# Seven-product blocks for one more unit, three wide sums for eight narrow ones, and output halves added in DRAM

## The chip, the cores and the metric

One NeuronCore of one Trainium2 chip runs the whole program. The metric is device time in microseconds (us). The kernel before takes 655.93 us, the median of three runs (655.39 to 657.26). In the text PE is the matrix engine, DVE the vector engine, ACT the scalar engine, POOL the GpSimd engine and SP the engine whose queue issues nearly all DMAs.

## The reference, cut to what matters

For each of 8 batches and 8 heads, 512 tokens `x` and 32 state rows attend to each other in both directions; the result, 4352 rows of 512, goes through a feed-forward block with a hard-swish:

```
xread = softmax(x @ state.T / 8) @ state        # 8 x 8 heads, 512 tokens
sread = softmax(state @ x.T / 8) @ x            # 8 x 8 heads, 32 rows
t = concat([xread, sread]) as (4352, 512)
h = t @ w_in                                    # (4352, 2048)
g = h * clip(h + 3, 0, 6) / 6
out = g @ w_out                                 # (4352, 512), float32
```

## The kernel before, in words

The hidden width 2048 is taken in two sweeps of 1024, that is 8 blocks of 128 each. A **unit** is one sweep over one batch's 512 tokens, or over the 256 rows of all `sread` (b = 8): 18 units of 8 **steps**. Unit order before: sweep 0 with b = 0 to 8, then sweep 1 with b = 0 to 8. Step n makes one 128-row block of h in a PSUM bank (`first`, tile `ps_h`, two banks): six matmuls of 512 columns, because every float32 factor is kept as a high and a low part and three products of parts are summed. ACT then writes relu(h + 3) (L1162 or L1177) and DVE multiplies min(that, 6) by h (L1164 or L1179).

What follows a step comes in two kinds. In a **plain** unit (`second`) g is split into high and low (`split`, L379 on ACT and L380 on DVE), and four row tiles are multiplied by a block of `w_out`: 4 x 3 matmuls of 512 columns a step (L988), summed over 8 steps in PSUM banks `acc0` to `acc3`. In a **seven-product** unit (`seven(k)`: sweep 1, b = 1 to 7) two g blocks and two row tiles form a 2 x 2 block matrix, multiplied by seven half-size products for eight (`seconds`): 7 x 3 matmuls of 256 columns a step (L1077). Four `w_out` combinations are made once (`combine`, in sweep 1's unit b = 0). For each step DVE makes four 128-wide sums and differences of quarters of G (L1045), and the quarters (tile `g_hi`, `g_lo`) and three sums (tile `tmp`) are split. A unit has two passes (q = 0, 1) of four steps, two row tiles each; at the end of a pass the four banks are joined: ACT copies acc0 and part of acc1 out to `tops` (L1090, L1091), DVE adds three pieces into `ot` (L1094, L1097), POOL adds the rest in four instructions (L1100), and SP stores the half to `out` (L1112).

`ot` holds 1/6 of the sum over both sweeps: sweep 0 stores its part to a DRAM buffer (`part`, L1248) and sweep 1 loads it back (`load_part`, L1197). The two `sread` units are treated so too, the second one as the last unit of all.

The order of instructions is worked out while the program is built: `Plan` holds every operation with an engine, a cost, a rank (the table `RANKS`), dependencies and buffer slots, and lays them out engine by engine (`order`); engines run their rows strictly in that order. Idle transposes (L1433) fill the gaps of PE up to the first step.

Of the kernel before, what the change touches and what calls it, by code (L numbers as in the profile page):

```python
# [1463 lines left out]
```

## Time and profile before

| | before |
|---|---|
| median of 3 runs | 655.93 us |
| the profiled execution | 656.56 us, of which the span from first to last instruction 654.2 us |
| PE / DVE / ACT / POOL busy | 98% / 81% / 51% / 10% of the span |
| DMA | 82.00 MB moved |

The profiled execution lies 0.63 us above the median. Busy PE is not PE at its peak, since matmuls overlap: what tells is from which start to which start they come, and what an idle PE waited for. The stretch from 400 to 640 us is sweep 1 with its seven-product units; 120 to 400 us is most of sweep 0, the first `sread` unit and the one plain unit of sweep 1.

### The profile page before, as it was taken

What the parts mean: (1) busy time and instruction counts of PE and PEld (TensorE: products, weight loads), DVE (VectorE), ACT (ScalarE), POOL (GpSimd) and SP (SyncE); (2) the same over time, 40 slices, a digit from 0 to 9 for tenths busy, and PEclk for the clock granted to TensorE, in tenths of its full rate; (3) what the DMA queues carried; (4) which work ended last, traced back from release to release, by engine and by line L of the source; (5) the groups of instructions that cost most, each with busy time, mean ns of one, the idle gap of its engine ahead of it and who ended that gap; (6) DMA issues with size and microseconds to landing.
All of it is one profiled execution on the core that took longest, in us unless ns stands there. A gap on an engine that the chain in (4) does not pass through costs nothing.

```text
span 654.2 us, 11536 instructions
## 1 busy us (share of the span) xinstructions
PE 638.1 (98%) x4383; PEld 514.9 (79%) x4383; DVE 530.1 (81%) x1023; ACT 331.9 (51%) x591; POOL 63.3 (10%) x63
## 2 busy tenths in 40 slices
PE   8999998999999999999999999999999999999997
PEld 7446776867777868777897877988898889898996
DVE  4989779887979859788479557899899989899973
ACT  4848444554545634546355444454555454464531
POOL 0000000000000000000000000123121422313122
PEclk9999999999999999999999999999999999999999
DMA  9985796887859557333313032305040404020102
GB/s 288 266 188 148 126 223 105 247 168 182 173 149 225 126 145 176 88 74 141 90 65 134 32 134 76 123 33 181 18 166 34 165 33 166 34 97 33 65 34 64
DMA packets 147007, 82.00 MB, mean 125 GB/s; under 512 B 124808, under 2 KB 134536, under 8 KB 144776
## 3 DMA queue, kind: packets, MB, share of 16 engines
q1 hardware_dynamic: 146808, 81.01, 45.1%
q8 instruction: 34, 0.56, 0.3%
q10 hardware_dynamic: 144, 0.26, 0.2%
q14 instruction: 21, 0.17, 0.1%
HBM read 50.84 MB, written 26.74 MB: 119 GB/s over the span
## 4 chain that ended last, share of the span: by engine, by line
PE 79%; DVE 11%; SPq 4%; DMA 3%; issue 2%; ACT 1%; DVEq 0%; ACTq 0%
PE ps_h L988 26%; PE acc L988 25%; PE acc L1077 18%; PE ps_s L604 3%; PE acc L1212 2%; DVE g_lo L380 2%; SPq L591 2%; PE ps_s L988 2%; PE ps_h L604 1%; PE ps_h L1143 1%; SPq L559 1%; DVE g L1045 1%; DVE tmp L380 1%; DMA raw<-in_moe_w_in_dram 1%; DMA raw<-in_x_dram 1%
## 5 line engine op out<-in xcount | busy, mean ns | idle before, releaser
L988 PE MATMUL acc<-w_out_hi,g_hi 128*128 128x512 f32 x288 | 115.6, 401 | 0.9 <-ACT g_hi L379 0.9
L988 PE MATMUL acc<-w_out_hi,g_lo 128*128 128x512 f32 x288 | 112.3, 390 | 0.0
L988 PE MATMUL acc<-w_out_lo,g_hi 128*128 128x512 f32 x288 | 112.3, 390 | 0.0
L1177 ACT ACTIVATE g<-ps_h,three 128x512 f32<-128x512 f32 (+1 forms) x88 | 57.0, 649 | 78.9 <-PE ps_h L988 76.7
L1179 DVE SCALAR_TENSOR_TENSOR g<-g,ps_h 128x512 f32<-128x512 f32 (+1 forms) x88 | 55.7, 634 | 40.5 <-ACT g L1177 40.0
L1077 PE MATMUL acc<-w_out_hi,tmp 128*128 128x256 f32 x336 | 88.0, 283 | 0.0
L988 PE MATMUL ps_h<-aT_hi,wp_hi 128*128 128x512 f32 (+1 forms) x232 | 85.0, 366 | 2.4 <-DVE wp_lo L380 1.3
L988 PE MATMUL ps_h<-aT_lo,wp_hi 128*128 128x512 f32 (+1 forms) x232 | 83.8, 361 | 0.0
L988 PE MATMUL ps_h<-aT_hi,wp_lo 128*128 128x512 f32 (+1 forms) x232 | 83.5, 360 | 0.0
L1100 POOL TENSOR_TENSOR tops<-tops 128x256 f32<-128x256 f32 x28 | 23.5, 838 | 549.9 <-DVE g L1045 415.9
L379 ACT CAST g_hi<-g 128x512 fp32r<-128x512 f32 (+1 forms) x84 | 48.5, 579 | 46.7 <-PE acc L988 24.8
L988 PEld LDWEIGHTS acc<-w_out_hi,g_hi 128*128 128x128 f32 x288 | 54.1, 188 | 20.8 <-issue 6.9
L380 DVE TENSOR_TENSOR g_lo<-g,g_hi 128x512 fp32r<-128x512 f32 (+1 forms) x84 | 53.7, 640 | 19.8 <-ACT g_hi L379 17.3
L1077 PE MATMUL acc<-w_out_hi,g_lo 128*128 128x256 f32 x224 | 63.8, 285 | 1.7 <-DVE g_lo L380 1.7
L1077 PEld LDWEIGHTS acc<-w_out_hi,tmp 128*128 128x128 f32 x336 | 64.4, 192 | 0.1
L1077 PE MATMUL acc<-w_out_hi,g_hi 128*128 128x256 f32 x224 | 64.0, 286 | 0.3 <-DVE ot L1094 0.3
L988 PEld LDWEIGHTS acc<-w_out_hi,g_lo 128*128 128x128 f32 x288 | 54.1, 188 | 12.0 <-DVE g_lo L380 0.6
L1077 PE MATMUL acc<-w_out_lo,g_hi 128*128 128x256 f32 x224 | 63.4, 283 | 0.0
L988 PEld LDWEIGHTS acc<-w_out_lo,g_hi 128*128 128x128 f32 x288 | 54.1, 188 | 11.5 <-issue 1.1
L1162 ACT ACTIVATE G<-ps_h,three 128x512 f32<-128x512 f32 x56 | 38.4, 688 | 43.5 <-PE ps_h L988 43.5
L988 PEld LDWEIGHTS ps_h<-aT_hi,wp_hi 128*128 128x128 f32 x232 | 43.8, 189 | 11.2 <-issue 1.8
L988 PEld LDWEIGHTS ps_h<-aT_hi,wp_lo 128*128 128x128 f32 x232 | 43.8, 189 | 6.9
(153 smaller groups left out, 1273.1 us busy)
## 6 DMA issues: line engine op xcount, KB each, us to landing
part<-ot SPq DMA_DIRECT2D x8, 1024.0 KB, 4.7
ot<-part SPq DMA_DIRECT2D x8, 1024.0 KB, 6.9
raw<-in_x_dram SPq DMA_DIRECT2D x112, 64.0 KB, 3.3
xb<-in_x_dram SPq DMA_DIRECT2D x28, 256.0 KB, 4.8
out_dram<-ot SPq DMA_DIRECT2D x14, 512.0 KB, 2.8
raw<-in_moe_w_out_dram SPq DMA_DIRECT2D x11, 511.8 KB, 5.4
raw<-in_moe_w_in_dram SPq DMA_DIRECT2D x8, 511.0 KB, 5.1
raw<-raw SPq DMA_DIRECT2D x112, 32.0 KB, 2.0
```

The lines of the kernel that those rows point to most:

```text
L379: S_(cost, rank, lambda: nc.scalar.copy(hi(), src()), reads, [writes[0]])
L380: V(cost, rank, lambda: nc.vector.tensor_tensor(lo(), src(), hi().bitcast(F32), op=ALU.subtract), [*reads, writes[0]], [writes[1]])
L559: nc.sync.dma_start(x_tile(b, read)[:, :, j, :], x_v[b, j])
L591: nc.sync.dma_start(t[rows, i].rearrange("t (a c) -> t a c", c=NS), x[b, 4 * g + 2 * i + u, :, k * NS : (k + 1) * NS].rearrange("(a t) c - ...
L604: nc.tensor.matmul(out[u][cols, :], made["stT", b][rows, cols], moving(q)[rows], start=True, stop=True,)
L988: nc.tensor.matmul(ps, l, r, start=start and k == 0, stop=stop and k == n - 1)
L1077: nc.tensor.matmul(out, left(a, l), right(b, r), start=p == 0 and z == 0 and y == 0, stop=p == FPS // 2 - 1 and y == 2, skip_group_check=True)
L1100: add = lambda wide, out, a, b, reads, writes: ADDS(ADD_COST[wide], rank, lambda: ADD_ENGINE.tensor_tensor(out(), a(), b(), op=ALU.add), r ...
L1162: S_(0.68, n - 1.5, lambda: nc.scalar.activation(g(), bank(ps), AF.Relu, bias=three), [ps], [g_key], after)
L1177: S_(cost + 0.05, rank, lambda: nc.scalar.activation(g(), bank(ps)[:, :width], AF.Relu, bias=three), [ps], [g_key])
L1179: V(cost, rank, lambda: nc.vector.scalar_tensor_tensor(g(), g(), 6.0, bank(ps)[:, :width], op0=ALU.min, op1=ALU.mult), [ps], [g_key])
L1212: nc.tensor.matmul(bank(acc), made["g_hi", n][:, js], plain_out[f][1](), start=opens, stop=closes)
```

## The change

- The units' order: the two `sread` units stand in a row, between the sweeps, and their sums stay in the PSUM banks from one to the other, so the first is not copied out, stored and loaded again. The last unit is now sweep 1, b = 7.
- Sweep 1's b = 0 becomes a seven-product unit too. Of the last unit the second pass is plain (`seconds_of_last`), its two row tiles stored apart.
- Every second hidden block of sweep 1 has its sign turned: the weights are negated as they are unpacked, ACT's relu reads h with a factor of -1, and plain units turn the sign back while they split. With it the eight 128-wide sums of a pair of blocks become three (`quarter_sums`: 512, 256 and 256 wide), made for both passes at once. G is laid out by pass, so that a pass's quarters lie in a row.
- The join of a pass is one ACT instruction and five DVE instructions (`join`); POOL adds nothing.
- Sweep 0 stores its part to `out` itself, and each pass of sweep 1 is added to it in DRAM by a DMA that accumulates, issued from POOL (15 of them). Only the last unit's second half is still loaded and added on DVE. The tile `ot` of these units has one buffer, `po`, and a second one holds sums.
- A new table `RANKS`, some costs of the planner set anew, and a few operations tied to the one before of their kind.

The diff's core, with the table left out but for its first line:

```diff
@@ -22,115 +22,107 @@
 RANKS = [int(k) for k in """
-167 169 168 381 380 377 631 72 378 71 279 73 285 74 281 68 278 375 376 70 47 251 250 270 372 374 630 282 252 373 248
...
-    outp = ctx.enter_context(tc.tile_pool(name="outp", bufs=2))
+    outp = ctx.enter_context(tc.tile_pool(name="outp", bufs=1))
...
+            "po": 1, "sums": 4,
...
+        if negated:
+            first = S_(cost, rank, lambda: nc.scalar.mul(hi(), src(), -1.0), reads, [writes[0]], after)
...
-    units = [(s, b) for s in range(NCH // CPS) for b in range(B + 1)]
+    units = [(0, b) for b in range(B)] + [(0, B), (1, B)] + [(1, b) for b in range(B)]
...
-    seven = lambda k: units[k][0] and 0 < units[k][1] < B
+    seven = lambda k: units[k][0] and units[k][1] < B
+    turned_sign = lambda f: f >= FPS and f % 2 == 0
...
+    def quarter_sums(k, p, rank):
...
+        qs = slice(0, 1 if last else 2)
...
+        sum_of[k, p] = V(wide, rank, lambda: nc.vector.tensor_tensor(
+            to(0, 2), four()[:, :, 1:3], four()[:, :, 0:1].to_broadcast(list(four()[:, :, 1:3].shape)),
+            op=ALU.subtract), g_keys, [s_keys[0]], first_of["sums"] + chain)
+        V(half, rank, lambda: nc.vector.tensor_tensor(
+            four()[:, :, 0:1], to(0), four()[:, :, 2:3], op=ALU.add), [*g_keys, s_keys[0]], [less])
+        V(half, rank, lambda: nc.vector.tensor_tensor(
+            to(2), four()[:, :, 3:4], four()[:, :, 0:1], op=ALU.subtract), [*g_keys, less], [s_keys[1]])
...
-            sum_of[k * FPS + t, m] = SUMS(SUM_COST, rank - 2.5, lambda m=m, a=a, b=b, op=op, of=of: SUM_ENGINE.tensor_tensor(
-                of(m), of(a), of(b), op=op), g_keys + [(*s_key, r) for r in reads],
...
+        if q == 0:
+            quarter_sums(k, p, rank - 2.5)
...
-        S_(0.62, rank, lambda: nc.scalar.mul(spare(e_key), bank(acc[0]), 1.0 / 6.0), [acc[0]], [e_key])
...
+        S_(0.36, rank, lambda: nc.scalar.mul(E()[:, left_half], bank(acc[0])[:, left_half], -1.0 / 6.0),
+           [acc[0]], [e_key], first_of["sums"])
+
+        def join(cost, out, a, b, reads, writes):
+            V(cost, rank, lambda: nc.vector.scalar_tensor_tensor(
+                out(), a(), 1.0 / 6.0, b(), op0=ALU.mult, op1=ALU.add), reads, writes)
...
+        plan.add("P", 1.3, rank, lambda: nc.gpsimd.dma_start(
+            rows_of(units[k][1])[:, 2 * q : 2 * q + 2], ot_of(k)[:, 2 * q : 2 * q + 2], accum_op=ALU.add),
+            [*[(*o_key, 2 * q + r) for r in range(2)], ("part", units[k][1])], [], (), 1000.0, 256, 3.0)
...
+    def seconds_of_last(k, t):
...
+                product(bank(acc[r]), [
+                    ((a_half["hi"]()[:, i, rs], a_half["lo"]()[:, i, rs]),
+                     [w_out_of(h, FPS + 2 * p + i, 1)[:, 0, :] for h in ("hi", "lo")])
+                    for i in range(2)], p == 0, p == FPS // 2 - 1)
...
-        add(0, lambda: spare(e_key)[:, right_half], lambda: spare(e_key)[:, right_half],
-            lambda: spare(e_key)[:, left_half], [], [e_key])
...
+            Q(n + 3, 262.0 * nt, lambda: nc.sync.dma_start(rows_of(b), ot()), keys, [("part", b)], pieces=512)
```

How the rows move, at three places. In the changed file the lines are others: L380 is L384, L453 is L459, L467 is L477, L1164 is L1235, L1077 is L1110.

DVE, in the middle of a seven-product unit, around the end of a pass: G is a product block, `g` before holds sums, `acc` is a PSUM bank. Before:

```order
L1164 SCALAR_TENSOR_TENSOR G<-G,ps_h 128x512
L1045 TENSOR_TENSOR g<-g,G 128x128
L1045 TENSOR_TENSOR g<-G,g 128x128
L1164 SCALAR_TENSOR_TENSOR G<-G,ps_h 128x512
L1045 TENSOR_TENSOR g<-G 128x128
L1094 SCALAR_TENSOR_TENSOR ot<-acc_5429,ot 128x512
L1045 TENSOR_TENSOR g<-g,G 128x128
L1045 TENSOR_TENSOR g<-G,g 128x128
L380 TENSOR_TENSOR g_lo<-G,g_hi 128x512
L1097 SCALAR_TENSOR_TENSOR ot<-acc_5498,ot 128x256
L1045 TENSOR_TENSOR G<-G 128x128
```

The same place after; here `sums` holds the sums and `g` the joined pieces:

```order
L1235 SCALAR_TENSOR_TENSOR G<-G,ps_h 128x2x256
L1128 SCALAR_TENSOR_TENSOR g<-acc_5778,g 128x256
L1128 SCALAR_TENSOR_TENSOR ot<-acc_5793,g 128x512
L1128 SCALAR_TENSOR_TENSOR g<-acc_5793,g 128x256
L1128 SCALAR_TENSOR_TENSOR ot<-acc_5770,g 128x512
L1235 SCALAR_TENSOR_TENSOR G<-G,ps_h 128x2x256
L1065 TENSOR_TENSOR sums<-G 128x2x256
L1068 TENSOR_TENSOR G<-sums,G 128x2x128
L384 TENSOR_TENSOR g_lo<-G,g_hi 128x512
L384 TENSOR_TENSOR tmp<-sums,tmp 128x384 x2
L1070 TENSOR_TENSOR sums<-G 128x2x128
```

Many narrow sums gave way to a few wide ones, and a pass's join stands as a row of instructions that hang on one another.

POOL, all that it has to do up to its first additions before, and then all of it after:

```order
masks.py:197 MEMSET ident 128x128
L335 MEMSET sread_t 128x4x64
masks.py:199 ISA
masks.py:199 AFFINE_SELECT ident<-ident 128x128
L1100 TENSOR_TENSOR tops<-tops 128x256 x2
L1100 TENSOR_TENSOR ot<-ot,tops 128x512 x2
```

```order
masks.py:197 MEMSET ident 128x128
L327 MEMSET sread_t 128x4x64
masks.py:199 ISA
masks.py:199 AFFINE_SELECT ident<-ident 128x128
L1139 DMA out_dram<-ot 128x1024 x2
L1139 DMA out_dram<-ot 128x2x512 x13
```

Before, 56 additions stand on POOL (the two last rows repeat through sweep 1); after, none, and 15 DMA issues.

SP, the first loads of the program (`ot` is the first batch's x, `early` and `raw` are places for weights, `raw<-in_x_dram` a piece of the second batch's x). Before:

```order
L571 DMA ot<-in_x_dram 128x4x256 x2
L517 DMA st_raw<-in_state_dram 128x1x64 x2
L453 DMA early_105<-in_moe_w_in_dram 128x4x511 x2
L591 DMA raw<-in_x_dram 32x16x32
L453 DMA raw<-in_moe_w_out_dram 128x2047
L453 DMA early_131<-in_moe_w_in_dram 128x4x1023
```

After:

```order
L581 DMA ot<-in_x_dram 128x4x256 x2
L527 DMA st_raw<-in_state_dram 128x1x64 x2
L459 DMA raw<-in_moe_w_out_dram 128x2047
L601 DMA raw<-in_x_dram 32x16x32
L459 DMA early_109<-in_moe_w_in_dram 128x4x511 x2
L459 DMA early_112<-in_moe_w_in_dram 128x4x1023
```

A block of `w_out` and a piece of x now stand ahead of the first blocks of `w_in`.

## Rows read from the trace of the kernel before

**Rows 1.** Stretches: busy time (instructions) of each engine, PE clock, DMA share, GB/s.

```profile
core 0: us, PE busy (x) PEld busy (x) DVE busy (x) ACT busy (x) POOL busy (x), PEclk, DMA share, GB/s
0.00:20.00 20.00, 16.30 (x136) 13.66 (x137) 10.98 (x23) 9.72 (x19) 0.95 (x7) 1.00 0.93 299
...
120.00:400.00 280.00, 278.79 (x1771) 218.64 (x1770) 213.85 (x382) 140.39 (x240) 0.00 (x0) 1.00 0.50 131
400.00:640.00 240.00, 236.86 (x1755) 212.05 (x1754) 214.61 (x456) 121.51 (x226) 58.45 (x53) 1.00 0.24 86
```

**Rows 2.** Whom PE waited for from 395 us on: us in all, times, longest.

```profile
PE acc L1077 <- DVE g_lo L380: 1.7, 2, 1.1
PE ps_h L988 <- DVE G L1164: 0.8, 2, 0.5
PE ps_h L988 <- DVE wp_lo L380: 0.3, 1, 0.3
PE acc L1077 <- DVE ot L1094: 0.3, 1, 0.3
```

**Rows 3.** Timeline of PE near 457 us, across its longest wait.

```profile
456.64 0.28 PE L1077 MATMUL acc<-w_out_lo,g_hi 128*128 128x256 f32 x1
458.06 0.39 PE L1077 MATMUL acc<-w_out_hi,g_lo 128*128 128x256 f32 x1 [1.14 <-DVE g_lo L380]
```

**Rows 4.** The chain that ended last, three pieces: start, us, what, how many.

```profile
148.81 3.40 PE acc L988 x15
152.21 1.36 PE ps_h L988 x6
...
488.72 6.83 PE acc L1077 x57
```

**Rows 5.** Timeline of DVE, then of POOL, near 520 us: start, us, what.

```profile
520.36 1.38 DVE L1045 TENSOR_TENSOR G<-G 128x128 f32<-128x128 f32 x1
...
522.25 0.28 DVE L1045 TENSOR_TENSOR g<-g,G 128x128 f32<-128x128 f32 x1
...
519.89 1.69 POOL L1100 TENSOR_TENSOR ot<-ot,tops 128x512 f32<-128x512 f32 x1
```

**Rows 6.** Groups on DVE, 395 to 645 us: busy us, mean ns | idle.

```profile
L380 DVE TENSOR_TENSOR g_lo<-G,g_hi 128x512 fp32r<-128x512 f32 x56 | 40.5, 729 | 2.1 <-ACT g_hi L379 2.0
...
L380 DVE TENSOR_TENSOR tmp<-g,tmp 128x384 fp32r<-128x384 f32 x55 | 34.7, 636 | 2.2 <-ACT tmp L379 1.4 <-PE acc L1077 0.4
L1045 DVE TENSOR_TENSOR g<-G 128x128 f32<-128x128 f32 x55 | 20.4, 376 | 0.8
...
L1094 DVE SCALAR_TENSOR_TENSOR ot<-acc,ot 128x512 f32<-128x512 f32 x28 | 19.0, 685 | 2.9 <-PE acc L1077 2.4 <-issue 0.4
L1045 DVE TENSOR_TENSOR g<-G,g 128x128 f32<-128x128 f32 x55 | 17.4, 326 | 1.0
L1097 DVE SCALAR_TENSOR_TENSOR ot<-acc,ot 128x256 f32<-128x256 f32 x14 | 5.8, 417 | 0.9 <-PE acc L1077 0.8
```

**Rows 7.** Whom PE waited for in the first 395 us.

```profile
PE ps_h L988 <- DVE g L1179: 1.1, 2, 0.9
...
PE ps_h L988 <- DVE wp_lo L380: 1.0, 1, 1.0
PE acc L988 <- ACT g_hi L379: 0.9, 1, 0.9
PE ps_h L988 <- DVE wp L380: 0.8, 1, 0.8
```

**Rows 8.** Timeline of ACT at the program's start.

```profile
10.93 0.77 ACT L462 CAST tops<-early 128x512 f16<-128x512 bf16 x1 [0.46 <-DMA early<-in_moe_w_in_dram]
```

**Rows 9.** Timeline of DVE at the program's end.

```profile
649.51 0.69 DVE L1237 SCALAR_TENSOR_TENSOR ot<-ps_s,ot 128x512 f32<-128x512 f32 x1 [1.29 <-PE ps_s L988]
```

**Rows 10.** The page's DMA issues: how many, KB each, us to landing.

```profile
ot<-part SPq DMA_DIRECT2D x8, 1024.0 KB, 6.9
...
out_dram<-ot SPq DMA_DIRECT2D x14, 512.0 KB, 2.8
```

More of the change, by code (lines that the diff above doesn't have):

```diff
@@ L461, in upper @@
             out = out.rearrange("p q (f k) -> p q f k", k=2) if kind == "in" else out.rearrange("p (e k) -> p e k", k=2)
-            nc.scalar.copy(out[..., 1], digits(pieces().bitcast(BF16), 2, i))
+            top = digits(pieces().bitcast(BF16), 2, i)
+            if kind == "in" and turned_sign(k + i):
+                nc.scalar.mul(out[..., 1], top, -1.0)
+            else:
+                nc.scalar.copy(out[..., 1], top)
         def join(i):
@@ L571, in load @@
                 nc.sync.dma_start(raw()[:, hs], x[0, hs].rearrange("h (p j) d -> p h j d", j=J))
-            Q(rank, 524.288, load, writes=[(*raw_key, g)], pieces=512, late=0.0)
+            Q(rank, 524.288, load, writes=[(*raw_key, g)], pieces=512, late=0.6)
             if g == 0:
@@ L619, in wp_of @@
         if key[0] == "ot":
-            both = get(key, lambda: outp.tile([P, 2, NG, CH], F32R, name="wp", tag="ot"))
+            both = out_tile(key, [P, 2, NG, CH], F32R)
             return both[:, ("hi", "lo").index(half)]
@@ L1028, in combine @@
             [*keys, *places["hi"]], places["lo"])
+    def quarter_sums(k, p, rank):
+        last = k == len(units) - 1
+        qs = slice(0, 1 if last else 2)
+        g_keys = [("G", (k, p), i) for i in range(2)]
+        less, s_keys = ("G", (k, p), "less"), [("sums", (k, p), m) for m in range(2)]
+        four = lambda: whole(k, p).rearrange("p q i r e -> p q (i r) e")[:, qs]
+        to = lambda a, b=None: sums_of(k, p)[:, qs, a : b or a + 1]
+        wide, half = (0.34, 0.21) if last else (0.6, 0.34)
+        if "sums" not in first_of:
+            first_of["sums"] = [m for slot, users in plan.users.items() for m in users
+                                if slot[0] in ("ot", "top", "sread", "apart")]
+        chain = [sum_of[k, p - 1]] if p else [sum_of[k - 1, FPS // 2 - 1]] if k - 1 in range(B + 2, len(units)) else []
+        sum_of[k, p] = V(wide, rank, lambda: nc.vector.tensor_tensor(
[5 more added lines that the diff above has]
+            to(2), four()[:, :, 3:4], four()[:, :, 0:1], op=ALU.subtract), [*g_keys, less], [s_keys[1]])
     def seconds(k, t):
@@ L1181, in first @@
         if not in_32:
-            split(n, half["hi"], half["lo"], g, [g_key], [("g_hi", n), ("g_lo", n)], cost)
+            in_turn["hi"] = split(n, half["hi"], half["lo"], g, [g_key], [("g_hi", n), ("g_lo", n)], cost, turned, in_turn.get("hi", []))
     def tiles_of(k):
         return J if units[k][1] < B else B * NS // P
-    def part(k):
-        b = units[k][1]
-        return get(("part", b), lambda: kept.tile([P, tiles_of(k), DO], F32, name=f"part{b}"))
     def ot_of(k):
-        return get(("ot", ("o", k)), lambda: outp.tile([P, J, DO], F32, name="ot"))
+        if seven(k):
+            return out_tile(("po", k), [P, J, DO], F32, 0)
+        return out_tile(("ot", ("o", k)), [P, J, DO])
     def load_part(k, rank, after):
-        nt = tiles_of(k)
-        Q(rank, 262.0 * nt, lambda: nc.sync.dma_start(ot_of(k)[:, :nt], part(k)),
-          [("part", units[k][1])], [("ot", ("o", k), j) for j in range(nt)], after)
+        Q(rank, 524.0, lambda: nc.sync.dma_start(ot_of(k)[:, 2:], rows_of(units[k][1])[:, 2:]),
+          [("part", units[k][1])], [("po", k, j) for j in range(2, J)], after, pieces=256)
     def second(n):
@@ L1374, in tile_state_attention_then_hardswish_ffn @@
         n = k * FPS
-        if sweep:
+        if k == len(units) - 1:
             at(n + 3, lambda k=k, n=n: load_part(k, n + 3, [first_of[n + 3]]))
@@ L1393, in waiting @@
             if seven(k) and 0 <= t < FPS:
-                work.append(lambda k=k, t=t: seconds(k, t))
+                last = k == len(units) - 1 and t >= FPS // 2
+                work.append(lambda k=k, t=t, f=seconds_of_last if last else seconds: f(k, t))
         m = n - LAG
```

189 lines of the change are left out of this document (105 added, 84 removed), and 209 rows, old and new, of the table RANKS.

## The prediction

> **What bounds the kernel now.** I read the stretches first [rows 1]. The reader is to see that PE is busy 278.79 of 280 us from 120 to 400 us and 236.86 of 240 us from 400 to 640 us, at the full granted clock in both. So PE's own work makes the time, and a change can win only by fewer matmuls or by removing the short waits between them. The neighbour to look at is DVE: 213.85 of 280 us busy (76%) in the first of the two stretches, 214.61 of 240 us (89%) in the second, where POOL works too, 58.45 us.
>
> Then the list of whom PE waited for. From 395 us on it has six waits, all on DVE, 1.7 + 0.8 + 0.3 + 0.3 = 3.1 us [rows 2]. A wait costs more than it says. Across the longest one PE starts a matmul at 456.64 and the next at 458.06, 1.42 us for a spacing that is otherwise 0.12: 1.30 lost for a wait of 1.14, and the matmul behind it takes 0.39 in place of 0.28 [rows 3]. That is 0.16 + 0.11 = 0.27 us on top of each wait, so the six hold about 3.1 + 1.6 = 4.7 us. Before 120 us waits of other kinds stand; between 120 and 395 us only one, the 1.0 us on `wp_lo` [rows 7]. A DVE busy at 76% is thus nearly unseen by PE, one at 89% is not.
>
> The chain of waits gives PE's prices, from start to start: 15 matmuls of 512 columns in 3.40 us (0.227 each), 57 of 256 columns in 6.83 us (0.120 each), and six of `first` in 1.36 us [rows 4].
>
> **The change part by part.** *Matmuls.* Counted in the two orders, sweep 1's b = 0 turned into seven products and half a unit turned back into plain ones take 48 matmuls of 512 columns away and add 84 of 256: -48 x 0.227 + 84 x 0.120 = -10.9 + 10.1 = **-0.8 us**, all on PE's path. The rest of PE's work only changes place.
>
> *DVE in a seven-product unit.* A unit is 8 x 1.36 + 8 x 21 x 0.120 = 31 us of PE. Before, each of its eight half steps has four 128-wide sums, of which the longest kind takes 0.376 and the shortest 0.326 on average [rows 6]; with the two between them 1.44 us, 11.5 us a unit. After, each of four block pairs has one sum of 512 and two of 256 elements. The trace has no such sum on SBUF. One of 128 elements takes 0.28 alone [rows 5], and the joins of 256 and 512 take 0.417 and 0.685 [rows 6], which lies on one line with it; so I take 0.685 + 2 x 0.417 = 1.52, 6.1 us a unit, 5.4 less. The least would be no saving at all, if the broadcast and strided operands made the sums twice as long; nothing in the rows points to that. The join grows from 2 x 0.685 + 0.417 = 1.79 to 3 x 0.417 + 2 x 0.685 = 2.62 us a pass, with two passes +1.7 us a unit.
>
> *POOL's 56 additions go.* They cost DVE time: a sum took 1.38 us at 520.36 beside an addition that ran on POOL from 519.89 to 521.58, and 0.28 at 522.25 when POOL was done [rows 5]. The split of G, 0.729 on average beside them, would take about 0.685, and the one of `tmp`, 0.636, about 0.55, midway between 0.417 and 0.685 [rows 6]: 8 x 0.044 + 8 x 0.086 = 1.0 us a unit less. Together DVE has 5.4 - 1.7 + 1.0 = 4.7 us less in 31, and 89% becomes some 74%. That is the level of the stretch from 120 to 400 us, which has one wait in 280 us; over the 250 us of sweep 1 I leave one such wait, 1.0 + 0.27, say 1.2 us. The gain is 4.7 - 1.2 = **-3.5 us**. Ends: nothing gained, and all 4.7.
>
> *The joins' chain.* The five join instructions hang on one another, and what is queued behind them on DVE are the next G products and splits, which PE takes next. Hidden by DVE's 26% of free time; if that cover is too short at a pass's end, a wait of its bare overhead comes back (rival two).
>
> *Accumulating DMAs.* Sweep 1's part loads (1 MB, 6.9 us to landing) and 14 stores (512 KB, 2.8 us) [rows 10] become 15 DMAs of 512 KB that read, add and write. None stands in the trace. The nearest rows give 2.8 us, a plain store, to 2.8 + 6.9 = 9.7 us, as if a load of twice the size stood in front; I take 5, nearer the store, which has the same size and direction. The wait that this adds: the tile they are sent from has one buffer, so the first write of a unit's join waits on DVE for both DMAs of the unit before, and behind it on DVE queue G products and splits for PE. Between those points lies a pass, half a unit: 15.5 us, less the join that may be stretched to twice its busy 2.6 us, so about 10 us. It covers 5 and just covers 9.7: **0 us**.
>
> *The two `sread` units in a row, and `combine` beside the second.* One copy out, store and load go; the combinations of `w_out`, before beside a plain unit, now share DVE with narrower matmuls. Cover: DVE's lead over PE, which by the 76% is there. If it is gone, two waits like the longest, 2 x 1.42 = 2.8 us [rows 3]. Taken 0.
>
> *The start.* On SP a 512 KB block of `w_out` and a small piece of x pass two blocks of `w_in`. At 299 GB/s [rows 1] 0.5 MB is 1.7 us, and ACT waited 0.46 us for such a block at 10.93 [rows 8]. Ends: +1.7 if all of it is seen, -0.5 if the other order ends that wait; DVE is idle 9 of the first 20 us [rows 1], so I take 0.
>
> *The end.* As before a DVE instruction (0.69 us at 649.51 [rows 9]) and a store follow the last matmul: 0.
>
> **The sum** is made against the profiled execution, 656.56 us: 656.56 - 0.8 - 3.5 = 652.3. It lies 0.63 above the median, so 652.3 - 0.6 = **651.7 us** for the median.
>
> **Rivals.** *One, sweep 0 gains too.* New ranks may also clear the waits of the first 395 us: g, `wp_lo`, `g_hi`, `wp`, 1.1 + 1.0 + 0.9 + 0.8 = 3.8 us in five waits [rows 7], with overheads 5.1. Three of these gone: 651.7 - 3.1 = 648.6. For it: DVE has room there. Against: what waits there is first loads and first splits, and the order of sweep 0 is much the same.
>
> *Two, the waits move.* Fewer sums, but at each of 15 pass ends the join chain delays a split by the bare overhead: 15 x 0.27 = 4.1 us where the forecast leaves 1.2: 651.7 + 2.9 = 654.6. For it: two of the six waits are on `g_lo`, the split behind such a row [rows 2]. Against: the free time on DVE. A later start and middle (+1.7 and +2.8, 656.2) ends in the same band.
>
> *Three, POOL still disturbs DVE.* 15 DMA issues stand there in place of 56 additions. If one issue costs DVE what one addition does, 15/56 of the 4.7 us of waits stay, 1.3: 653.0. The trace has POOL slow DVE by additions only [rows 5]. The Trainium skill (GPSIMD Engine Reference, "Key points") says that GpSimd shares its SBUF interfaces with VectorE and that DVE instructions with two SBUF inputs contend; the sums of rows 5 agree, 1.38 against 0.28 us, and whether descriptors written by GpSimd do the same no run here shows.
>
> *Four, slower: the accumulation lands too late.* If a DMA that reads, adds and writes lands later than the 10 us that the single buffer leaves, DVE stands at the first write of seven units' joins, with PE's next splits behind it. At 12 us that is 7 x 2 = 14 us: 665.7. It decides from 10 us on. For it: two transfers' worth in one, just inside by the upper bound of 9.7 [rows 10]. Against: DMA engines are only 0.24 busy then [rows 1]. The Trainium skill (DMA: Bandwidth & Descriptors, "Anatomy of one DMA — SWDGE (gpsimd) path") fits 2.0 us and bytes over 436 GB/s for a DMA from GpSimd, by which 512 KB would take an estimated 3.2 us and this rival would fall; its fit is not told to be of accumulating ones, and no row here shows one.
>
> **How the numbers follow.** The forecast, 651.7, gets 0.50, with its own range 649.5 to 654 (the waits' ends and the start's). Rival one 0.14, two with the late start 0.20, three 0.06, four 0.10. About 0.3%, 2 us, is what a measurement of this kernel can tell from no change, so below 654.0 is faster and above 657.9 slower: the forecast, one and three are faster, 0.70; two is the same, 0.20; four is slower, 0.10. The range of 8 in 10 takes in one and two and leaves out four and the far part of one: 647.5 to 656.8.
>
> **What would show it.** Right: no additions on POOL; DVE's share in the middle of sweep 1 near 74%, sums of 256 elements near 0.42 us, one to three waits of PE there and about 1 us in all; accumulating DMAs landing in 3 to 8 us, no DVE wait on them at a join; first step of PE within 1 us of where it was. Wrong: PE waits of 0.1 to 0.5 us at each pass's end (two); DVE instructions still stretched near POOL's issues (three); DVE waiting for a DMA once a unit (four); a first step over 1 us late. The sum fails if DVE's share falls and PE's waits do not.

## The result and the profile after

The changed kernel takes 648.6 us, the median of four runs (647.05 to 650.55), beside 656.46 us for the kernel before in four runs (655.39 to 657.26): a ratio of 0.9883, with a 95% interval of 0.9851 to 0.9915. That is 7.9 us less; the forecast was 4.2 us less, 651.7 us. The time lies on the forecast's side and in the range of 8 in 10 (647.5 to 656.8), but 0.9 us below the forecast's own range (649.5 to 654), and the gain is nearly twice as large. The profiled execution of the changed kernel took 647.05 us with a span of 645.3 us, 1.5 us under its median, while that of the kernel before was 0.1 us over the median of its four runs. So the two traces stand 8.9 us apart in their spans, which says about a microsecond more than the medians do.

The stretches of the changed kernel, with the columns of [rows 1]:

```profile
120.00:400.00 280.00, 279.66 (x1846) 222.59 (x1845) 219.99 (x394) 144.79 (x252) 0.00 (x0) 1.00 0.50 123
400.00:640.00 240.00, 240.00 (x1761) 215.73 (x1760) 190.91 (x358) 112.59 (x212) 17.40 (x15) 1.00 0.31 60
```

From 400 to 640 us PE is busy all 240.00 us, where it had 236.86; no wait of PE is left in the list of this stretch, so there is no row to show for [rows 2]. DVE has gone from 89% to 80% (190.91 of 240), not to the 74% of the forecast. Of the waits of the first 395 us [rows 7] those on DVE's g and `wp` are gone and `g_hi` and `wp_lo` are shorter, but new ones on ACT stand there, the longest on `w_in`:

```profile
PE ps_s L770 <- ACT w_in L710: 1.7, 1, 1.7
...
PE acc L998 <- ACT g_hi L383: 0.6, 1, 0.6
PE ps_h L998 <- DVE wp_lo L384: 0.3, 1, 0.3
```

The groups of DVE from 395 to 636 us, as in [rows 6]:

```profile
L384 DVE TENSOR_TENSOR g_lo<-G,g_hi 128x512 fp32r<-128x512 f32 x58 | 39.2, 686 | 2.7 <-ACT g_hi L383 2.0 <-PE acc L1110 0.3
...
L384 DVE TENSOR_TENSOR tmp<-sums,tmp 128x384 fp32r<-128x384 f32 x57 | 30.7, 553 | 9.9 <-PE acc L1110 7.1 <-ACT tmp L383 2.8
L1128 DVE SCALAR_TENSOR_TENSOR ot<-acc,g 128x512 f32<-128x512 f32 x30 | 20.5, 688 | 1.2 <-PE acc L1110 0.6
L1128 DVE SCALAR_TENSOR_TENSOR g<-acc,g 128x256 f32<-128x256 f32 x45 | 18.9, 421 | 7.8 <-ACT g L1124 4.7 <-PE acc L1110 2.4
L1065 DVE TENSOR_TENSOR sums<-G 128x512 f32<-128x512 f32 x25 | 17.1, 689 | 0.6
L1068 DVE TENSOR_TENSOR G<-sums,G 128x256 f32<-128x256 f32 x25 | 10.5, 422 | 0.5
L1070 DVE TENSOR_TENSOR sums<-G 128x256 f32<-128x256 f32 x25 | 10.4, 423 | 0.5
```

The prices that the forecast put on operations it had not seen were right: a sum of 512 elements takes 0.689 us (0.685 taken), one of 256 takes 0.422 (0.417), the split of G 0.686 and that of `tmp` 0.553 without POOL's additions (0.685 and 0.55). The accumulating DMAs, with the store of the part from SP beside them (columns of [rows 10]):

```profile
out_dram<-ot SPq DMA_DIRECT2D x8, 1024.0 KB, 5.2
out_dram<-ot POOLq DMA_DIRECT2D x15, 512.0 KB, 6.0
```

They land in 6.0 us in the median, inside the bounds of 2.8 and 9.7 and near the 5 that was taken. The 15 differ, though:

```profile
DMA to landing us min/median/max: 5.4/6.0/9.5
```

The longest, 9.5 us, is the one issued at 490.74. By the Trainium skill (DMA: Bandwidth & Descriptors, "Anatomy of one DMA — SWDGE (gpsimd) path") 512 KB would have been an estimated 3.2 us; the measurement decides against it for this kind of DMA. The shortest way from an issue to the first write of the next unit's join, POOL's row first and DVE's behind it:

```profile
620.20 1.20 POOL L1139 DMA_DIRECT2D out_dram<-ot  x1 [9.42 <-DVE ot L1128]
...
629.31 0.68 DVE L1128 SCALAR_TENSOR_TENSOR ot<-acc,g 128x512 f32<-128x512 f32 x1
```

That is 9.1 us; in the other six units it is 10.9 to 15.1, where the forecast had "about 10". DVE waits for a DMA at none of the joins. The narrowest place is another one: behind the DMA of 490.74 the next write starts at 501.59, 10.85 us after the issue and 1.4 us after that DMA's landing. The end, as in [rows 9]:

```profile
641.35 0.69 DVE L1179 SCALAR_TENSOR_TENSOR ot<-acc,ot 128x512 f32<-128x512 f32 x1 [3.39 <-PE acc L998]
642.07 0.37 ACTq L1182 DMA_DIRECT2D out_dram<-ot  x1
```

DVE's last instruction takes the same 0.69 us. But from its start to the end of the span it is 645.3 - 641.35 = 4.0 us, before 654.2 - 649.51 = 4.7. This is 0.7 us that the forecast set at 0. Both last stores are 256 KB from ACT's queue; the one before goes to `sread` rows, which lie in pieces of the output, the one after to 128 rows in a row. That fits the 0.7 us but was not tried alone.

### The profile page after: what moved, and what is told of

It reads as the page before. It is cut to its first block, busy times and chain, and to the rows that moved or that the text cites. A ratio compares the mean times of both kernels' runs of the same rounds, so it can differ in the third digit from the quotient of the medians.

```text
span 645.3 us, 11398 instructions
## 1 busy us (share of the span) xinstructions
PE 634.2 (98%) x4422; PEld 515.2 (80%) x4422; DVE 508.3 (79%) x931; ACT 324.8 (50%) x585; POOL 18.4 (3%) x22
## 4 chain that ended last, share of the span: by engine, by line
PE 86%; DMA 5%; SPq 4%; DVE 2%; ACT 2%; issue 0%; DVEq 0%; ACTq 0%
PE ps_h L998 27%; PE acc L998 27%; PE acc L1110 24%; PE ps_s L614 3%; DMA early<-in_moe_w_out_dram 2%; PE ps_h L614 2%; PE acc L1281 1%; SPq L601 1%; DMA raw<-in_x_dram 1%; SPq L569 1%; DMA raw<-in_moe_w_out_dram 1%; DMA early<-in_moe_w_in_dram 1%; PE ps_h L955 1%; PE ps_h L1213 1%; ACT tops L472 1%; SPq L534 0%
## 5 line engine op out<-in xcount | busy, mean ns | idle before, releaser
L1249 ACT ACTIVATE g<-ps_h,three 128x512 f32<-128x512 f32 (+1 forms) x80 | 51.2, 645 | 76.9 <-PE ps_h L998 64.7
L1110 PE MATMUL acc<-w_out_hi,tmp 128*128 128x256 f32 x360 | 89.0, 284 | 0.0
L1233 ACT ACTIVATE G<-ps_h,three 128x512 f32<-128x512 f32 x64 | 44.2, 691 | 68.4 <-PE ps_h L998 66.5
L1252 DVE SCALAR_TENSOR_TENSOR g<-g,ps_h 128x512 f32<-128x512 f32 (+1 forms) x80 | 50.0, 629 | 36.3 <-ACT g L1249 35.6
L998 PEld LDWEIGHTS acc<-w_out_hi,g_hi 128*128 128x128 f32 x288 | 54.1, 188 | 19.2 <-issue 7.2
L1110 PEld LDWEIGHTS acc<-w_out_hi,tmp 128*128 128x128 f32 x360 | 66.6, 192 | 3.0 <-issue 1.7
L1110 PE MATMUL acc<-w_out_hi,g_hi 128*128 128x256 f32 x240 | 68.2, 284 | 0.0
L1110 PE MATMUL acc<-w_out_lo,g_hi 128*128 128x256 f32 x240 | 67.9, 283 | 0.0
L1110 PE MATMUL acc<-w_out_hi,g_lo 128*128 128x256 f32 x240 | 67.9, 283 | 0.0
L1235 DVE SCALAR_TENSOR_TENSOR G<-G,ps_h 128x512 f32<-128x512 f32 x64 | 43.7, 686 | 20.8 <-ACT G L1233 20.1
L384 DVE TENSOR_TENSOR g_lo<-g,g_hi 128x512 fp32r<-128x512 f32 (+1 forms) x72 | 45.2, 641 | 10.7 <-ACT g_hi L383 9.0
L383 ACT CAST g_hi<-g 128x512 fp32r<-128x512 f32 (+1 forms) x72 | 40.8, 583 | 22.8 <-DVE g L1252 14.9
L1110 PE MATMUL acc<-w_out_lo,tmp 128*128 128x256 f32 x180 | 50.9, 283 | 0.0
L1110 PEld LDWEIGHTS acc<-w_out_hi,g_hi 128*128 128x128 f32 x240 | 45.9, 191 | 4.7 <-issue 2.5
```

Source lines behind the costliest of these rows:

```text
L383: first = S_(cost, rank, lambda: nc.scalar.copy(hi(), src()), reads, [writes[0]], after)
L384: V(cost, rank, lambda: nc.vector.tensor_tensor(lo(), src(), hi().bitcast(F32), op=ALU.subtract), [*reads, writes[0]], [writes[1]])
L998: nc.tensor.matmul(ps, l, r, start=start and k == 0, stop=stop and k == n - 1)
L1110: nc.tensor.matmul(out, left(a, l), right(b, r), start=p == 0 and z == 0 and y == 0, stop=p == FPS // 2 - 1 and y == 2, skip_group_check=True)
L1233: S_(0.68, n - 1.5, lambda: nc.scalar.activation(g(), by_pass(), AF.Relu, bias=three, scale=-1.0 if turned_sign(FPS + i) else 1.0), [ps], ...
L1235: V(0.63, n - 1.5, lambda: nc.vector.scalar_tensor_tensor(g(), g(), 6.0, by_pass(), op0=ALU.min, op1=ALU.mult), [ps], [g_key])
```

## The experiments

Theory one was the forecast's: DVE's load made the six waits, and fewer sums lighten it most, POOL's absence second. The rivals were the order (of sweep 0, or of the rows in sweep 1) and the stretching of single instructions. Times are medians; kernels measured together stand beside the same runs of the kernel before: 655.74 us for the first four, 656.57 for the next four, 656.22 for the last three.

### POOL's additions alone

`b_nopool`, in the kernel before:

```diff
-        add = lambda wide, out, a, b, reads, writes: ADDS(ADD_COST[wide], rank, lambda: ADD_ENGINE.tensor_tensor(
-            out(), a(), b(), op=ALU.add), reads, writes)
+        add = lambda wide, out, a, b, reads, writes: ADDS(ADD_COST[wide], rank, lambda: None, reads, writes)
```

> The kernel before, without the four additions of each join on POOL (so the output lacks these pieces); all else stands. Theory one, DVE's load makes the six late waits and POOL's additions are a large part of that load: the narrow sums fall from 0.33 to 0.38 to about 0.28 us, the splits of G from 0.73 to 0.69 and of tmp from 0.64 to 0.55, DVE in the middle of sweep 1 goes from 89% to about 78%, and of the 4.7 us that the waits cost 3 to 5 go: 651.5 to 653.5 us. Rival, the waits come from the order of the rows and not from the load: DVE gets faster all the same, the waits on it stay, 655 to 657 us.

Measured: 650.23 us, a ratio of 0.9917 (0.9904 to 0.9929), 5.5 us less. The stretch from 400 to 640 us, and two groups of DVE:

```profile
400.00:640.00 240.00, 240.00 (x1794) 217.44 (x1779) 194.96 (x462) 124.20 (x230) 0.00 (x0) 1.00 0.24 88
```

```profile
L380 DVE TENSOR_TENSOR g_lo<-G,g_hi 128x512 fp32r<-128x512 f32 x56 | 38.2, 687 | 4.8 <-ACT g_hi L379 4.5
...
L1045 DVE TENSOR_TENSOR g<-G 128x128 f32<-128x128 f32 x55 | 15.6, 288 | 0.8
```

DVE is at 81%, PE at 240.00 of 240, and a narrow sum takes 0.288 us where it took 0.376 [rows 6]. Nothing but the 56 additions is gone, and with them all waits of sweep 1 and about two thirds of the whole gain. In the kernel before neither PE nor DVE waits for POOL in this stretch, so it is not the additions' results that they waited for.

How the additions reach PE shows in front of the longest wait [rows 3]. The kernel before, POOL's row first, then three of DVE's; the last one makes the `g_lo` that PE waits for:

```profile
452.93 1.29 POOL L1100 TENSOR_TENSOR ot<-ot,tops 128x512 f32<-128x512 f32 x1
...
453.04 1.33 DVE L1045 TENSOR_TENSOR g<-G,g 128x128 f32<-128x128 f32 x1
...
455.64 1.11 DVE L380 TENSOR_TENSOR tmp<-g,tmp 128x384 fp32r<-128x384 f32 x1
...
457.33 0.68 DVE L380 TENSOR_TENSOR g_lo<-G,g_hi 128x512 fp32r<-128x512 f32 x1
```

The same three in `b_nopool`:

```profile
451.44 0.29 DVE L1045 TENSOR_TENSOR g<-G,g 128x128 f32<-128x128 f32 x1
...
453.14 0.55 DVE L380 TENSOR_TENSOR tmp<-g,tmp 128x384 fp32r<-128x384 f32 x1
...
454.26 0.69 DVE L380 TENSOR_TENSOR g_lo<-G,g_hi 128x512 fp32r<-128x512 f32 x1
```

From the join's third piece on DVE (451.95 and 450.79) to this `g_lo` it is 5.4 us with the additions and 3.5 without: 1.9 us of delay, of which PE sees 1.14 as a wait.

### The eight narrow sums back in the changed kernel

`a_narrow` makes the sums of a pair of blocks 128 wide again; the code of the first of them:

```diff
-        sum_of[k, p] = V(wide, rank, lambda: nc.vector.tensor_tensor(
-            to(0, 2), four()[:, :, 1:3], four()[:, :, 0:1].to_broadcast(list(four()[:, :, 1:3].shape)),
-            op=ALU.subtract), g_keys, [s_keys[0]], first_of["sums"] + chain)
+        sum_of[k, p] = V(wide, rank, lambda: narrow((
+            (t_of(0), f_of(1), f_of(0), ALU.subtract), (t_of(1), f_of(2), f_of(0), ALU.subtract))),
+            g_keys, [s_keys[0]], first_of["sums"] + chain)
```

> The changed kernel, with its three wide sums of a pair of blocks cut into the eight 128-wide ones that they replaced, in the same places. Each pair costs 8 x 0.29 = 2.3 us in place of 1.53, 3.2 us a unit, so DVE goes from 80% to about 90% of the middle of sweep 1, as in the kernel before. Theory one, load alone makes the waits: 3 to 5 us of PE waits come back, 651.5 to 653.5 us. Rival, the order leaves PE enough lead that a DVE at 90% is not seen: within 1 us of the changed kernel, 648 to 649.5 us.

Measured: 649.08 us, a ratio of 0.9896 (0.9879 to 0.9913); beside the changed kernel's 0.9883 (0.9851 to 0.9915) no difference that can be told, which leaves the wide sums a worth of 0 to some 3 us.

```profile
400.00:640.00 240.00, 239.98 (x1761) 215.61 (x1760) 197.13 (x485) 114.01 (x214) 17.41 (x15) 1.00 0.30 59
```

```profile
L1068 DVE TENSOR_TENSOR sums<-G 128x128 f32<-128x128 f32 x162 | 37.2, 285 | 0.5
```

DVE rises to 82% only, not to 90%. The reader can see why in the group: 162 x 0.285 is 46.2 us, but the busy time is 37.2. In the records narrow sums that do not hang on one another run partly over one another, and the product of count and mean counts that twice. All eight sums of a pair together keep DVE busy for 47.6 us here (216 sums from 395 to 645 us, 0.22 each); in `b_nopool`, where more of them hang on the one before, for 56.9 (220 sums, 0.26 each). So the fewer sums were worth 6.2 us of DVE in this stretch, not the 20 and more that were expected, and nothing on PE that can be told. This run therefore doesn't test a DVE at 90%; the next one does.

### A DVE as busy as before, without POOL

`b_nopool_load` is `b_nopool` with twelve sums a unit made twice:

```diff
+            times = 2 if m == 0 or m == 2 and q else 1
...
-            of(m), of(a), of(b), op=op), g_keys
+            of(m), of(a), of(b), op=op) for _ in range(times)], g_keys
```

> The kernel before without POOL's additions (the output lacks them), and with the first sum of every half step, and the third one of each second pass, made twice: twelve more narrow sums a unit, some 3 us, so that DVE is as busy as in the kernel before (88 to 91% of the middle of sweep 1) without anything on POOL. Theory one, the load alone makes the waits: 3 to 5 us come back, 653 to 655.5 us. Rival, what hurts is that single instructions are stretched up to five times where PE is just waiting for them, and an evenly spread load does not: 650 to 651 us.

Measured: 652.68 us, a ratio of 0.9946 (0.9926 to 0.9967).

```profile
400.00:640.00 240.00, 239.19 (x1785) 216.09 (x1770) 214.63 (x542) 124.17 (x229) 0.00 (x0) 1.00 0.24 86
```

DVE is busy 214.63 us, to a fiftieth of a microsecond the 214.61 of the kernel before [rows 1]. Yet PE idles 0.8 us here and 3.1 there, and the time lies between `b_nopool` and the kernel before. So neither theory has it alone: the load as such brings back 1.9 us of the 5.5 by the two ratios (2.4 by the medians), a loose figure, since the two intervals meet. Firmer is the other side: this kernel is 2.2 to 4.9 us faster than the kernel before at the same busy time, and that part needs POOL's additions at work.

### The additions on DVE in place of POOL

`b_adds_dve` is the smallest edit that frees POOL and keeps the sum whole:

```diff
-    ADDS, ADD_ENGINE, ADD_COST = G_, nc.gpsimd, (0.85, 1.45)
+    ADDS, ADD_ENGINE, ADD_COST = V, nc.vector, (0.4, 0.68)
```

> The kernel before with the 56 additions of its joins on DVE in place of POOL, the smallest edit that takes POOL away without the rest of the change. DVE gets 14 x (2 x 0.42 + 2 x 0.69) = 31 us more and loses the contention: some 93% of the middle of sweep 1. By the run with doubled sums (89% busy, no POOL, 2.5 us over the one without additions) the load brings back 2.5 to 5 of the 5.5 us: 652.5 to 655.5 us, still not slower than before. Rival, at 93% DVE becomes the bound of the stretch and the waits outgrow the old ones: 657 us or more.

Measured: 663.84 us, a ratio of 1.0119 (1.0088 to 1.0149): slower. The stretch, and whom PE waited for from 395 us on:

```profile
400.00:640.00 240.00, 232.42 (x1698) 207.09 (x1683) 213.91 (x502) 119.91 (x220) 0.00 (x0) 0.99 0.24 86
```

```profile
PE ps_h L988 <- DVE G L1164: 3.9, 5, 1.6
PE acc L1077 <- DVE ot L1094: 1.9, 2, 1.5
```

The rival holds: PE now waits for the joins and for the G products queued behind them, 7.6 us of idle time in this stretch alone. DVE's share is 89% as in the kernel before and in `b_nopool_load`, and PE idles 7.6 us where it idled 3.1 and 0.8. So the share does not say what PE loses; where the work stands does, and here PE's waits name the join's rows and what is queued behind them. Taking POOL's work away pays only if it does not land on DVE, and that is what the changed join and the accumulating DMAs are for: a join of 2.6 us of DVE where this one has 1.8 + 2.2.

### POOL's additions put back into the changed kernel

`a_pool` adds, behind each accumulating DMA:

```diff
+            for w in 6 * (256,):
+                nc.gpsimd.tensor_tensor(scratch[:, :w], ot(1)[:, :w], ot(0)[:, :w], op=ALU.add)
```

> The changed kernel, with six additions of 256 elements on POOL behind each accumulating DMA, about 5 us a pass as before the change, into a scratch tile that nobody reads. DVE's instructions with two inputs in SBUF are slowed beside them as in the kernel before: 2 to 3.5 us a unit more, DVE at 86 to 90%. Theory one, the removal of POOL's additions is a large part of the gain: 1.5 to 4 us come back, 650 to 652.5 us. Rival, POOL's additions did no harm to the time: 648 to 649.5 us.

Measured: 666.79 us, a ratio of 1.0164 (1.0149 to 1.0179). The additions cost 18 us, far over what was expected. The stretch, then DVE near 523 us with POOL's row last, then two groups:

```profile
400.00:640.00 240.00, 230.22 (x1666) 203.45 (x1666) 215.68 (x339) 108.37 (x202) 87.50 (x94) 0.99 0.27 53
```

```profile
523.66 1.22 DVE L1066 TENSOR_TENSOR sums<-G 128x512 f32<-128x512 f32 x1
524.81 0.95 DVE L1071 TENSOR_TENSOR sums<-G 128x256 f32<-128x256 f32 x1
...
527.44 0.68 DVE L385 TENSOR_TENSOR wp_lo<-ps_h,wp_hi 128x512 fp32r<-128x512 f32 x1
...
523.13 5.81 POOL L1144 TENSOR_TENSOR scratch<-ot 128x256 f32<-128x256 f32 x6
```

```profile
L385 DVE TENSOR_TENSOR g_lo<-G,g_hi 128x512 fp32r<-128x512 f32 x56 | 47.8, 865 | 0.3 <-ACT g_hi L384 0.2
...
L1240 DVE SCALAR_TENSOR_TENSOR G<-G,ps_h 128x512 f32<-128x512 f32 x56 | 38.0, 683 | 11.6 <-ACT G L1238 11.2
```

POOL adds from 523.13 to 528.94. Beside it a sum of 512 takes 1.22 us for 0.689 and one of 256 takes 0.95 for 0.422, while instructions that read PSUM keep their time: `wp_lo` from PSUM 0.68 at 527.44, the G product 0.683 on average, as ever. The split of G, with two operands in SBUF, goes from 0.686 to 0.865 on average. The Trainium skill (GPSIMD Engine Reference, "Key points") says the same of DVE instructions with two SBUF inputs, and these rows agree. PE idles 9.8 of the 240 us. POOL's 87.5 us contain the DMA issues; the additions alone take 85.4 us in the whole program, 5.7 a pass, for 62.5 or 4.5 a pass in the kernel before. That is a quarter more a pass, but the loss is three times as large. The rest is put down to the place, right behind the join, where the sums of both passes and the splits stand in a row; place and amount were not tried apart.

`a_narrow_pool` has both edits, the narrow sums and the additions on POOL.

> The changed kernel with eight narrow sums for its three wide ones and with the six additions of 256 elements on POOL behind each accumulating DMA. With the wide sums these additions cost 18 us, three times what POOL's additions cost in the kernel before. If the width is to blame (a wide sum beside POOL holds DVE up to 1.5 us in front of the splits that PE needs): 652 to 658 us. If it is the place (POOL's work starts right behind the join, where the changed order has the splits and the sums of both passes) and the amount (5.8 us a pass for 4.5): 663 to 668 us.

Measured: 678.98 us, a ratio of 1.0335 (1.0297 to 1.0373), over both ranges that were expected, so width is not to blame. It is the other way round:

```profile
L1069 DVE TENSOR_TENSOR sums<-G 128x128 f32<-128x128 f32 x155 | 57.4, 425 | 0.4
```

A narrow sum goes from 0.285 to 0.425 us, and eight of them hold DVE longer (some 3.4 us a pair) than three wide ones in `a_pool` (0.89 + 0.60 + 0.65 = 2.1 us on average). Here the wide sums do pay, 11 to 12 us: they are an insurance against a neighbour that this kernel no longer has.

### The accumulating DMAs

`a_spstore`:

```diff
-        plan.add("P", 1.3, rank, lambda: nc.gpsimd.dma_start(
-            rows_of(units[k][1])[:, 2 * q : 2 * q + 2], ot_of(k)[:, 2 * q : 2 * q + 2], accum_op=ALU.add),
+        plan.add("P", 1.3, rank, lambda: nc.sync.dma_start(
+            rows_of(units[k][1])[:, 2 * q : 2 * q + 2], ot_of(k)[:, 2 * q : 2 * q + 2]),
```

> The changed kernel with a plain store from SP in place of each accumulating DMA from POOL (so the output has sweep 1's part alone in these rows). Theory one, the accumulation is free, since it lands within the pass that the one buffer leaves: 648 to 649.5 us, as the changed kernel. Rival three of the prediction, an issue on POOL disturbs DVE, or the accumulation holds something: 647 us or less.

Measured: 648.15 us, a ratio of 0.9863 (0.9840 to 0.9885), against 0.9883 (0.9851 to 0.9915) for the changed kernel; the intervals overlap for the most part.

```profile
400.00:640.00 240.00, 240.00 (x1763) 215.79 (x1762) 192.43 (x361) 114.12 (x215) 0.00 (x0) 1.00 0.17 59
```

Without a DMA on POOL, DVE has 192.43 us and with them 190.91. A wide sum takes 0.689 us in both. The issues, 1.16 us each on POOL by the profile's count, do not disturb DVE, and the accumulation is free as far as these runs can tell: by the ratios the plain stores are 1.3 us faster, within the intervals.

`a_two` sends each DMA twice:

```diff
+            for _ in range(2):
+                nc.gpsimd.dma_start(
+                    rows_of(units[k][1])[:, 2 * q : 2 * q + 2], ot_of(k)[:, 2 * q : 2 * q + 2], accum_op=ALU.add)
```

> The changed kernel with each accumulating DMA sent twice, the second waiting for the first (so sweep 1's part is added twice): the one buffer comes free some 14 to 15 us after a join's end in place of 7.2. From issue to the first write of the next unit's join the changed kernel's trace has 9.1 to 15.1 us. Rival four of the prediction at its full price: 1 to 5 us of DVE waits in five of seven units, 12 to 15 us in all, and PE loses the same: 660 to 663 us. Against it, DVE's free 20% and the blocks of G made ahead take most of it up: waits of DVE on the DMA show, PE loses 0 to 4 us, 648 to 652.5 us.

Measured: 659.12 us, a ratio of 1.0043 (1.0015 to 1.0072), 10.5 us over the changed kernel. At one place (POOL's two issues, then DVE), then the waits of DVE and of PE on this chain:

```profile
493.26 1.19 POOL L1141 DMA_DIRECT2D out_dram<-ot  x1 [5.49 <-DVE ot L1128]
502.02 1.20 POOL L1141 DMA_DIRECT2D out_dram<-ot  x1 [7.58 <-DMA out_dram<-ot]
...
507.87 0.69 DVE L1128 SCALAR_TENSOR_TENSOR ot<-acc,g 128x512 f32<-128x512 f32 x1 [3.68 <-DMA out_dram<-ot]
```

```profile
DVE ot L1128 <- DMA out_dram<-ot: 8.0, 4, 3.7
```

```profile
PE ps_h L998 <- DVE G L1238: 3.2, 1, 3.2
PE acc L998 <- DVE ot L1128: 2.9, 1, 2.9
```

The second DMA is issued at 502.02, and the first write of the next unit's join starts at 507.87, after 3.68 us of waiting: 14.6 us behind the first issue, as expected (each DMA takes 6 to 9 us here from its issue to the point that frees the next). DVE waits 8.0 us in all and PE 6.1, about half of the full price of 12 to 15. The 20% of DVE's time that is free does not help there, because what PE needs next is queued behind the waiting instruction. The 10.5 us are more than these waits. From PE's last matmul to the end it is 5.0 us here and 4.4 in the changed kernel, with the second DMA of the last pass issued as late as 646.93. And the mean granted clock of the ten runs is 0.980 to 0.995, lowest in the slowest run (663.87 us), where the changed kernel's four have 0.994 to 1.000, so part of the 10.5 us can be PE's clock.

### The order of sweep 0

`b_order0` forced the kernel before into the changed kernel's order through dependencies among the planner's operations:

```diff
+            for row in ORDER:
+                row = [int(n) for n in row.split()]
+                for n, then in zip(row, row[1:]):
+                    self.ops[then][4].add(n)
```

> The kernel before, with the order of sweep 0 (all operations that the planner puts into the first 280 us, on all five queues) taken from the changed kernel; sweep 1 keeps its old kind of work. Theory one: the 2.9 us that the changed kernel's PE stands less before 400 us are the order's alone, so 653 to 654 us, with the waits at 98 and 141 us gone. Rival: they hang on something else that changed (the store of the part to the output, the sign in the weights), the order is worth nothing, 655.5 to 657 us.

Measured: 688.64 us, a ratio of 1.0505 (1.0485 to 1.0526). This was a fault of the experiment: a dependency makes the planner reckon with the whole latency of the operation before, a DMA's landing included, so it planned gaps that do not exist and filled them with 176 idle transposes for 38. What the order itself is worth it does not show. The stretch from 120 to 400 us:

```profile
120.00:400.00 280.00, 266.78 (x1727) 206.38 (x1726) 206.12 (x368) 131.87 (x226) 0.00 (x0) 0.97 0.52 130
```

Besides the late start, PE waits 7.5 us for DMAs, is busy 266.78 of the 280 us, and the granted clock of the stretch averages 0.97.

`b_ord` gives the planner the order itself (an operation of the list is taken only when it is the next on its engine):

```diff
+                    if n in line_of and line_of[n][-1] != n:
+                        continue
```

> The kernel before with sweep 0 in the changed kernel's order on all engines and queues, the idle transposes at the start and the planner's costs of these operations included (the first try forced the order through the planner's waits and so put 113 more idle transposes ahead of the first step). Sweep 1 with its POOL additions stays. Theory, the order of sweep 0 is worth the part of the gain that POOL's additions do not explain: 1 to 2 us, 653.7 to 654.7 us. Rival, the order is worth nothing that can be measured and the rest comes from the last store and the matmuls: 655 to 656.5 us.

Measured: 656.50 us beside 656.57, a ratio of 0.9991 (0.9977 to 1.0005). Whom PE waited for, from the first 395 us and then from the rest:

```profile
PE ps_h L1067 <- DVE wp_lo L459: 1.5, 1, 1.5
PE acc L1067 <- ACT g_hi L458: 1.1, 2, 0.7
```

```profile
PE acc L1156 <- DVE g_lo L459: 1.7, 2, 1.2
PE ps_h L1067 <- DVE G L1243: 0.9, 2, 0.5
```

The rival holds: the order of sweep 0 gives nothing that can be measured in the median. The waits change their places (the ones on DVE's g and `wp` go, `wp_lo` grows to 1.5 us) and those of sweep 1 stay nearly as in [rows 2].

The median may hide two things that cancel. The profiled execution of `b_ord`, at a mean granted clock of 1.000, took 654.04 us, and PE's first step starts at 31.5 us in it, as in the changed kernel's (31.7), for 33.5 in the kernel before. But 8 of the 12 runs of `b_ord` have a mean granted clock of 0.992 to 0.995, and so have three of the changed kernel's four (0.994 to 0.995), while the 20 runs of the kernel before beside them have 0.998 to 1.000. Where such a run loses its clock shows in the trace of `a_spstore` further up, which has the same start:

```profile
10.00:20.00 10.00, 9.52 (x88) 7.46 (x89) 7.81 (x14) 5.53 (x10) 0.00 (x0) 0.66 1.08 346
```

For part of these 10 us PE's clock stood at the lower of its two levels (1.2 for 2.4 GHz), and the first step starts at 33.3 us. In the 10 us before, PE was busy 6.32 us, and 6.54 in the changed kernel's trace, where the clock stays at 1.00. So the new order starts PE's steps 1 to 2 us earlier at the full clock (32.7 to 33.5 us in the traces with the old one), and a lower clock at the start can take that back. What the order is worth without that, one run at 1.000 does not settle, and what makes the clock fall in some runs is not shown.

`b_ord_nopool` is `b_ord` with POOL's additions left out.

> Both at once: sweep 0 in the changed kernel's order, and the four additions of each join on POOL left out (the output lacks these pieces). If the two add up and are nearly the whole gain: 648.5 to 649.5 us, within 1 us of the changed kernel. If the order is worth nothing: 650 to 650.7 us, as without POOL's additions alone.

Measured: 650.45 us, a ratio of 0.9901 (0.9879 to 0.9923), the same as `b_nopool` within the intervals. So the additions are worth 5.5 to 6 us with either order, and the order nothing beside them.

## Why the prediction was right, and where it was not

**Side and mechanism** were right: PE bound, DVE's waits in sweep 1, their end in a DVE with more room. No wait moved to the pass ends (rival two), and sweep 0's order gave nothing in the median (rival one): `b_ord` puts it at 0, with 1.5 us as the most that its interval leaves.

**That the range held the time was in part luck.** The measured 648.6 us lies under the forecast's own range, whose lower end is 649.5. What took the wider range down to 647.5 was rival one, and its 648.6 meets the measured time to the tenth. But the mechanism of that number, waits of sweep 0 cleared by new ranks, gave nothing in the median; of the 3.1 us between 651.7 and 648.6, 2.0 came out of sweep 1's waits and 0.7 out of the program's end.

**The step that fell short is the size of the wait term**, -3.5 us. It gave the six waits 4.7 us and left one wait of 1.2 in place; `b_nopool`, in which nothing else changes, puts the term at 5.5 us, with 6.0 between the two kernels in the new order. The price of the six was right: from the starts of PE's matmuls, against spacings of 0.227 and 0.120, they lose 4.7 us, 0.10 to 0.11 of it each time in the spacing behind the wait. Two things lie beside it. The first is the one wait kept, 1.2 us: the level of 76% in sweep 0 was read as if a wait belonged to the load, but at 80 to 82% sweep 1 has none. The second is what the list of waits does not show, six delays of 0.04 to 0.24 us, 0.9 us in all. One of them, two matmuls 0.26 us apart for 0.12:

```profile
624.29 0.28 PE L1077 MATMUL acc<-w_out_lo,g_hi 128*128 128x256 f32 x1
624.55 0.39 PE L1077 MATMUL acc<-w_out_hi,g_lo 128*128 128x256 f32 x1
```

None of the twelve delays stands in `b_nopool`. 3.5 + 1.2 + 0.9 = 5.6 us, for 5.5 measured. (The list of [rows 7] also has a second wait between 120 and 395 us, 0.2 us on g, beside the one that the prediction names.)

**Where the room comes from was mis-told.** The forecast booked 5.4 us a unit on fewer sums and 1.0 on POOL. But its 11.5 us for the narrow sums came from averages that contain POOL's disturbance: with POOL idle they take 32 x 0.288 = 9.2 us, so 2.3 of the 5.4 belonged to POOL. And narrow sums overlap in the records, so count times mean was too much: by busy time a unit's narrow sums take 10.6 us in the kernel before and 8.3 in `b_nopool`, and the wide ones 6.1. The runs put the gain on POOL: without its additions 5.5 us, with the narrow sums back no loss that can be told. In the sum the two entries were added, so that the mistake did not show in it.

**DVE's share** came to 80% for 74%. The sums gave 10.6 - 6.1 = 4.5 us a unit for 5.4, with the join's +1.7 and the splits' -1.0 as forecast; and the same 240 us now hold more work, 54 products of 512 where they held 49 and 6 of 256. A share also was not what PE's loss goes by: at 89%, PE idled 0.8 us (`b_nopool_load`), 3.1 (the kernel before) and 7.6 (`b_adds_dve`). The forecast knew load alone. Of the 5.5 us, load of equal size spread over the units brings back about 2; the rest needs POOL's additions, and the rows before the longest wait show how: they stretch the instructions that stand in front of what PE needs. That all of the rest comes about so is not shown.

**The terms set at 0**: the accumulation cost nothing that can be told (`a_spstore`), with a landing of 6.0 us for 5; POOL's issues were 0 (rival three falls); the end was -0.7 in place of 0. The first step came 1.8 us earlier, outside the 1 us that was to show the forecast right, and `b_ord` finds no worth of it in the median. The two `sread` units in a row were not tried alone. **The matmuls**, -0.8, were not tried alone either, but the two pages bear out the count: 4383 and 4422 records on PE, of which 38 and 41 idle transposes, so 36 more as -48 + 84 says. What the changed kernel has over `b_nopool`, 0.9883 against 0.9917 or about 2 us with intervals that meet, has room for this term and the end, 1.5 us, and is not settled further.

**Rival four** did not happen but was rightly built: with the DMAs doubled, the write of the join came 14.6 us after the first issue, DVE and PE lost about half of what the sum said, and the kernel became slower than the one before. Of the seven units of the changed kernel's trace one comes within 1.4 us of it: its DMA landed after 9.5 us, near the forecast's upper bound of 9.7, and the next join's write started 10.85 us after the issue.

No version among the runs beats the changed kernel by more than its interval; `a_narrow` equals it with simpler sums.

## What to carry to other kernels

When an engine shares its SBUF operands with another, look up what single instructions take with the neighbour at work and with it idle before putting a saving down to fewer instructions: an average that contains the disturbance books the neighbour's part under the wrong name. Work taken off POOL is a gain only where it does not go to the engine that PE waits for; a DMA that adds in DRAM is such a place, as long as it lands before its buffer is wanted. And count times mean is no busy time where short instructions overlap. A busy share does not say what the bound engine loses: that hangs on which instructions stand in front of what it needs next.
